# One query tile in the opening, one bounds test at a group's end, and two key tiles of values a visit, in an attention and bilinear-GLU block

## The chip, the cores and the metric

The kernel runs on one core of a Trainium2 chip. The metric is the device time of one execution in microseconds; times are compared as medians of several executions on the same chip. Engines are called as in the profile: PE is TensorE (PEld its weight loads), DVE is VectorE, ACT is ScalarE, POOL is GpSimd, SP is SyncE, which issues all of this kernel's DMAs.

## What is computed

A pre-norm attention with one shared head of keys and values, followed by a pre-norm bilinear GLU, both with a residual. In the reference, cut to what matters:

```python
B, S, D, H, Dh, F = 1, 2048, 576, 32, 18, 4608
q = (ln(x) @ wq).reshape(B, S, H, Dh).transpose(0, 2, 1, 3)
k, v = ln(x) @ wk, ln(x) @ wv                       # one head for all 32
scores = einsum("bhqd,bkd->bhqk", q, k) * Dh ** -0.5
o = einsum("bhqk,bkd->bhqd", softmax(scores), v)
h = x + o.transpose(0, 2, 1, 3).reshape(B, S, H * Dh) @ wo
n = ln(h)
out = h + ((n @ w_gate) * (n @ w_up)) @ w_down
```

## The kernel before

The 2048 rows are taken in four blocks of 512 queries (`TB`), the keys in 16 tiles of 128 (`NT`), the 32 heads in 8 groups of 4 (`NG`). The order of the work is written out by hand; each engine runs its own instructions in the order in which the program emits them, and semaphores hold an instruction until what it reads has been written and the buffer that it writes has been read.

`keys_values` (L141 to L295) is the opening. It loads x, normalises it block by block (`stats`, `scale`, `apply`), transposes each block on PE (`turn`, L200), splits it into a high and a low part (`parts`), projects keys and values (`project`, L220) and finishes the keys (`keys`, L231 to L235). `wq` is split in the same way by `split_wq`. The first block's five tiles of queries (`queries(0)`, 14 matmuls of 128 rows each, L307) stand between these steps.

`queries(b)` (L298) makes the queries of a block in five tiles of up to 7 heads. For the later blocks each of a tile's 14 steps is two matmuls of 64 rows, into two accumulators `psq` and `psr` (L316); DVE adds the two (L322, L323), splits the sum and stores it to DRAM (`q_dram`, L328, L329). `ps_f`, the pool of these accumulators, has two buffers. `bounds` (L336) computes from the absolute values of a block's queries and keys a bound for each query and head of the scores, which is subtracted inside the score matmul; it goes through `m_dram`. `guard` (L348) tests if the largest bound is above a limit; all engines read the flag, and only where it is set the branch computes exact maxima (`exact_maxima`). There are two guards: one for block 0 ahead of the first pair, one for the other blocks.

A pair (`pair`, L434) is two heads against one key tile: two score matmuls (L443) into a buffer `s`, and one exponential on ACT (L445) into a tile `P`. The pool of `s` has two buffers, that of `P` six (`P_BUFS`), later seven. Two pairs make a group's four heads against one key tile; `flush` (L454) multiplies them with the values, four matmuls side by side into `acc` (L460). `load_q`, `load_m` and `prefetch_q` bring a group's queries and bounds back from DRAM. At a group's end `normalise` (L478) turns the sums and divides, `chunk` transposes them, `project(b, c)` (L532) multiplies by `wo`; `run_aux` emits one of these per round.

The first attention's main loop is in `run` (L772 to L781). One visit emits a pair, steps of the other blocks' queries (`STEP` 2, each step counting 1, so two of them), a second pair, one round of `run_aux`, and flushes all waiting key tiles but the newest. When the queries are done and the second guard has run, the visits go on without them (L784 to L788) to the end of block 0's 256 pairs; then `fill` puts further pairs beside the output projection and the second normalisation. From `ffn(0)` (L658) on, the remaining pairs of the 1024 stand between the matmuls of the feed-forward, 8 to each of its 36 hidden tiles.

Of the kernel before, what the change touches and what calls it, by code (L numbers as in the profile page):

```python
# [22 lines left out]
P = 128  # L23
# [32 lines left out]
class Block:  # L56
# [84 lines left out]
    def keys_values(self):  # L141
        pe, act, dve, sp, pool = self.pe, self.act, self.dve, self.sp, self.nc.gpsimd
        with self.tc.tile_pool(name="p0", bufs=1) as p0:
            kvw = self.op.tile([P, S + 5 * P], F32, tag="ob", name="kvw")
            kv, wkv = kvw[:, 0:S], kvw[:, S:].rearrange("p (c m) -> p c m", c=5)
            x01 = [self.hp.tile([P, NQ, D], F32, tag="h", name=f"x{b}") for b in range(2)]
            x23 = self.otp.tile([P, 2, NQ, D], F32, tag="oT", name="x23")
            xs = x01 + [x23[:, 0], x23[:, 1]]
            wqr = [(self.qp if c < 2 else self.qb).tile([P, D], F32, tag="q" if c < 2 else "qs", name=f"wqr{c}")
                   for c in range(4)]  # L150
            for b in range(NB):
                for s in range(NQ):
                    sp.dma_start(xs[b][:, s, :], self.x[b * TB + s * P: b * TB + (s + 1) * P, :])
                if b == 0:
                    sp.dma_start(self.C, self.cst)
                    sp.dma_start(wkv, self.wkv)
                if b == 2:
                    for c in range(4):
                        sp.dma_start(wqr[c], self.wq[:, c, :])
            wqr.append(self.qp.tile([P, D], F32, tag="q", name="wqr4"))  # L160
            sp.dma_start(wqr[4], self.wq[:, 4, :])
            w_h = self.pp.tile([P, 5, P], F32R, tag="P", name="w_h")
            w_l = self.pp.tile([P, 5, P], F32R, tag="P", name="w_l")
            pool.memset(self.V, 0.0)
            pool.memset(self.V[:, :, 0:1], 1.0)
            ksum = p0.tile([P, NB], F32, name="ksum")
            mv = p0.tile([P, NT, 2], F32, name="mv")
            nmean, nmb, kab, kabq = (p0.tile([P, 1], F32, name=n) for n in ("nmean", "nmb", "kab", "kabq"))
            kabs = p0.tile([P, NB], F32, name="kabs")
            ma, mb, mc = (self.C[0:64, c:c + 1] for c in (C_MA, C_MB, C_MC))  # L170
            rs, xhs, trs = {}, {}, []

            def stats(lo, hi):
                for j in range(lo, hi):
                    b, s = divmod(j, NQ)
                    self.ln_stats(xs[b][:, s, :], mv[:, j, :], s, f"a{b}")

            def scale(lo, hi, eng):
                r = self.rstd(mv[:, lo:hi, 1], f"a{lo}", eng, hi - lo)
                n = self.lp.tile([P, hi - lo], F32, tag="n", name=f"n{lo}")  # L180
                eng.tensor_tensor(n, mv[:, lo:hi, 0], r, ALU.mult)
                eng.tensor_scalar(n, n, -1.0, None, ALU.mult)
                for j in range(lo, hi):
                    rs[j] = r[:, j - lo:j - lo + 1], n[:, j - lo:j - lo + 1]

            def apply(b):
                for s in range(NQ):
                    xh = xhs[s] = self.pp.tile([P, 640], F32, tag="P", name=f"xh{b}_{s}")
                    r, n = rs[NQ * b + s]
                    act.activation(xh[:, 0:D], xs[b][:, s, :], AF.Identity, bias=n, scale=r)  # L190
                    pool.tensor_copy(xh[:, D:], xh[:, 512:D])

            def turn(b):

                tail = self.ps_m(f"trt{b}")
                for r in range(2):
                    tr = self.ps_s(f"tr{b}_{r}").rearrange("p a (c q) -> p (a c) q", q=2 * P)
                    for s in (2 * r, 2 * r + 1):
                        for c in range(5):
                            pe.transpose(tr[:, c, (s - 2 * r) * P:(s - 2 * r + 1) * P] if c < 4 else tail[:, s * P:(s + 1) * P],  # L200
                                         xhs[s][:, c * P:(c + 1) * P], self.ident)
                        del xhs[s]
                    trs.append((b, r, tr))
                trs.append((b, None, tail))

            def parts():

                while trs:
                    b, r, tr = trs.pop(0)
                    XT = self.XT[b]  # L210
                    if r is None:
                        self.split_tail(XT[:, 8, :], tr)
                    else:
                        sl = slice(2 * r * P, (2 * r + 2) * P)
                        self.split(XT[:, 0:4, sl], XT[:, 4:8, sl], tr)

            def project(b):
                psk = self.ps_a(f"psk{b}")
                for i, (w, m) in enumerate(passes(w_h, w_l, self.XT[b])):
                    pe.matmul(psk, w, m, start=(i == 0), stop=(i == 13))  # L220
                act.activation(kv[:, b * TB:(b + 1) * TB], psk, AF.Copy, accum_out=ksum[:, b:b + 1])

            def keys(b):

                sl = slice(b * TB, (b + 1) * TB)
                if b == 0:
                    dve.tensor_scalar(nmean, ksum[:, 0:1], -1.0 / TB, None, ALU.mult)
                    dve.scalar_tensor_tensor(nmb[0:64], nmean[0:64], mb, mc, ALU.mult, ALU.add)
                kk = self.pp.tile([P, 2, TB], F32R, tag="P", name=f"kk{b}")
                hi, k2 = kk[0:64, 0], f32(kk[0:64, 1])  # L230
                act.activation(hi, kv[0:64, sl], AF.Identity, bias=nmean[0:64])  # L231
# [3 lines left out]
                dve.tensor_reduce(kabs[0:64, b:b + 1], f32(self.kT[0:64, sl]), AX.X, ALU.max, apply_absolute_value=True)  # L235

            first = self.queries(0)

            def first_queries():
                for _ in range(14):  # L240
                    next(first)

            def split_wq(c):
                act.copy(self.wq_h[:, c], wqr[c])
                pool.tensor_tensor(self.wq_l[:, c], wqr[c], f32(self.wq_h[:, c]), ALU.subtract)

            stats(0, 4)
            scale(0, 4, dve)
            apply(0)
            stats(4, 8)  # L250
            scale(4, 8, pool)
            turn(0)
            stats(8, 10)
            parts()
            split_wq(0)
            apply(1)
            stats(10, 12)
            scale(8, 12, pool)
            split_wq(1)
            turn(1)  # L260
            stats(12, 16)
            scale(12, 16, pool)
            self.split(w_h, w_l, wkv)
            project(0)
            parts()
            apply(2)
            for c in (2, 3, 4):
                split_wq(c)
            turn(2)
            project(1)  # L270
            parts()
            keys(0)
            apply(3)
            turn(3)
            parts()
            first_queries()
            keys(1)
            project(2)
            first_queries()
            first_queries()  # L280
            keys(2)
            project(NB - 1)
            first_queries()
            keys(NB - 1)
            first_queries()
            psv = self.ps_a("psv")
            for t in range(NT):
                pe.transpose(psv[:, t * 32:t * 32 + DH], kv[64:64 + DH, t * P:(t + 1) * P], self.ident[64:64 + DH, 64:64 + DH])
            dve.tensor_reduce(kab[0:64], kabs[0:64], AX.X, ALU.max)
            psb = self.ps_m("psb")  # L290
            pe.matmul(psb[:, 0:1], self.C[0:64, C_SEL:C_SEL + P], kab[0:64], start=True, stop=True)
            dve.tensor_copy(kabq, psb[:, 0:1])
            dve.tensor_scalar(self.G, self.C[:, C_G:C_G + 64], kabq, None, ALU.mult)
            drain(first)
            act.copy(self.V[:, :, 1:1 + DH], psv.rearrange("p (t c) -> p t c", c=32)[:, :, 0:DH])  # L295
# [52 lines left out]
    def guard(self, blocks, name):  # L348
# [10 lines left out]
        for _ in range(4):  # L359
            yield STEP  # L360
# [551 lines left out]
```

## Time and profile before

| | us |
|---|---|
| median of 3 runs | 2430.37 (2430.13 to 2431.2) |
| profiled execution | 2431.05, its span 2428.9 |
| PE busy | 2365.0, 97% of the span |
| ACT busy | 1241.3, 51% |
| DVE busy | 978.8, 40% |
| opening, to the first pair | 0 to 89.6 |
| first attention, to the feed-forward | 89.6 to 437 |
| feed-forward with pairs, then without | 437 to about 1914, about 1914 to 2428.9 |

A row of the timeline gives the start in us from the span's start, the duration, the engine, the source line, the operation, the tile written and the tiles read, the shape, how many instructions were merged (x), and in brackets how long the engine had been idle and what ended that. Matmuls overlap: a row's duration is longer than the time from its start to the next one's, and only the latter adds up. In the counts of L460 a tile of values is x8 (four matmuls, each executed in two passes). A row of a table by stage gives for each engine the busy time and the number of instructions, then the granted PE clock, the DMA share and GB/s.

### The profile page before, as it was taken

What the parts mean: (1) busy time and instruction counts of PE and PEld (TensorE: products, weight loads), DVE (VectorE), ACT (ScalarE), POOL (GpSimd) and SP (SyncE); (2) the same over time, 40 slices, a digit from 0 to 9 for tenths busy, and PEclk for the clock granted to TensorE, in tenths of its full rate; (3) what the DMA queues carried; (4) which work ended last, traced back from release to release, by engine and by line L of the source; (5) the groups of instructions that cost most, each with busy time, mean ns of one, the idle gap of its engine ahead of it and who ended that gap; (6) DMA issues with size and microseconds to landing.
All of it is one profiled execution on the core that took longest, in us unless ns stands there. A gap on an engine that the chain in (4) does not pass through costs nothing.

```text
span 2428.9 us, 44073 instructions
## 1 busy us (share of the span) xinstructions
PE 2365.0 (97%) x18778; PEld 1659.3 (68%) x18778; DVE 978.8 (40%) x1679; ACT 1241.3 (51%) x1396; POOL 354.8 (15%) x409
## 2 busy tenths in 40 slices
PE   5899989999999999999999999999999999999999
PEld 4433424576667667776767776767767778888888
DVE  5222224243334344443333344433333464554454
ACT  4588877746565655556465546466564401111110
POOL 4000000111111111111111111111111112222221
PEclk8899999999999999999999999999999999999999
DMA  3322130312211222422122122232221213423321
GB/s 114 113 64 67 56 112 18 97 57 72 72 62 59 85 62 62 147 67 70 45 73 71 62 62 80 87 113 77 67 67 45 79 65 104 146 89 103 98 89 59
DMA packets 68694, 190.59 MB, mean 78 GB/s; under 512 B 7720, under 2 KB 7848, under 8 KB 68488
## 3 DMA queue, kind: packets, MB, share of 16 engines
q1 hardware_dynamic: 68488, 187.66, 24.4%
q8 instruction: 152, 2.49, 0.4%
q14 instruction: 54, 0.44, 0.1%
HBM read 159.39 MB, written 19.40 MB: 74 GB/s over the span
## 4 chain that ended last, share of the span: by engine, by line
PE 83%; DVE 1%; ACT 1%; issue 0%; ACTq 0%; DVEq 0%
PE pg L678 23%; PE y L651 19%; PE acc L460 15%; PE gu L678 12%; PE s L443 9%; PE yo L547 3%; PE pu L678 1%; PE pt L486 1%; ACT P L445 1%; PE to L134 0%; PE tx L596 0%; DVE ws L86 0%; DVE hf L697 0%; ACT g L693 0%; DVE bsb L100 0%
## 5 line engine op out<-in xcount | busy, mean ns | idle before, releaser
L445 ACT ACTIVATE P<-s 128x1024 f32<-128x1024 f32 x1024 | 1034.2, 1025 | 654.5 <-PE s L443 567.4
L678 PE MATMUL pg<-X,ws 64*128 64x512 f32 x2538 | 700.3, 393 | 0.0
L678 PE MATMUL pu<-X,ws 64*128 64x512 f32 x2538 | 700.3, 393 | 0.0
L678 PEld LDWEIGHTS pg<-X,ws 64*128 64x128 f32 x2538 | 469.7, 186 | 108.1 <-issue 6.5
L460 PE MATMUL acc<-P,V 128*32 128x512 f32 x4096 | 492.6, 600 | 0.7 <-ACT P L445 0.6
L678 PEld LDWEIGHTS pu<-X,ws 64*128 64x128 f32 x2538 | 469.3, 186 | 4.1
L651 PE MATMUL y<-wds,ha 128*128 128x288 f32 x2304 | 465.4, 297 | 2.7 <-ACT ha L85 1.2
L443 PE MATMUL s<-q,kT 56*128 56x512 f32 x2048 | 435.9, 423 | 16.1 <-DVEq L365 12.8
L651 PEld LDWEIGHTS y<-wds,ha 128*128 128x128 f32 x2304 | 369.6, 188 | 26.8 <-issue 23.5
L443 PEld LDWEIGHTS s<-q,kT 56*128 56x128 f32 x2048 | 194.2, 185 | 218.5 <-ACT P L445 114.0
L651 PE MATMUL y<-wds,hl 128*128 128x288 f32 x1152 | 340.8, 296 | 0.1
L678 PE MATMUL gu<-X,ws 64*128 64x512 f32 x2700 | 314.3, 390 | 2.2 <-DVE ws L86 2.2
L85 POOL CAST ws<-wr 128x1152 fp32r<-128x1152 f32 x144 | 166.0, 1153 | 965.6 <-PE pu L678 684.8
L678 PEld LDWEIGHTS gu<-X,ws 64*128 64x128 f32 x2700 | 252.7, 185 | 58.3 <-issue 3.4
L460 PEld LDWEIGHTS acc<-P,V 128*32 128x32 f32 x4096 | 114.1, 109 | 246.4 <-issue 231.8
L697 DVE TENSOR_TENSOR hf<-pu,g 128x512 f32<-128x512 f32 x94 | 65.0, 691 | 528.8 <-ACT g L693 528.8
L653 DVE TENSOR_TENSOR h<-h,y 128x288 f32<-128x288 f32 x384 | 172.9, 453 | 257.3 <-PE y L651 257.1
L693 ACT COPY g<-gu 128x512 f32<-128x512 f32 x50 | 29.3, 587 | 389.4 <-PE gu L678 389.4
L85 POOL CAST wds<-wdr 128x576 fp32r<-128x576 f32 x144 | 146.2, 1034 | 510.3 <-PE y L651 503.4
L651 PEld LDWEIGHTS y<-wds,hl 128*128 128x128 f32 x1152 | 216.8, 188 | 0.4 <-DVE hl L86 0.4
L86 DVE TENSOR_TENSOR ws<-wr,ws 128x1152 fp32r<-128x1152 f32 x144 | 205.8, 1429 | 0.0
L86 DVE TENSOR_TENSOR hl<-hf,ha 128x512 fp32r<-128x512 f32 x144 | 100.8, 700 | 149.4 <-ACT ha L85 149.4
(144 smaller groups left out, 1272.7 us busy)
## 6 DMA issues: line engine op xcount, KB each, us to landing
wr<-in_wgu_dram SPq DMA_DIRECT2D x144, 576.0 KB
wdr<-in_wd_dram SPq DMA_DIRECT2D x144, 288.0 KB
q<-q_dram SPq DMA_DIRECT2D x64, 216.0 KB
q_dram<-qs SPq DMA_DIRECT2D x16, 504.0 KB
X<-X SPq DMA_DIRECT2D x28, 256.0 KB
x<-in_x_dram SPq DMA_DIRECT2D x16, 288.0 KB
h<-in_x_dram SPq DMA_DIRECT2D x16, 288.0 KB
out_dram<-h SPq DMA_DIRECT2D x16, 288.0 KB
```

Of the source, the lines that this page charges most:

```text
L85: (copy or self.cast)(hi, src)
L86: self.dve.tensor_tensor(lo, src, f32(hi), ALU.subtract)
L443: self.pe.matmul(s_[:, i], self.kT[o:o + 56, t * P:(t + 1) * P], self.q[o:o + 56, pr], start=True, stop=True)
L445: self.act.activation(p_, s_, AF.Exp, scale=SCALE)
L460: self.pe.matmul(self.acc[32 * j:32 * j + 32, :], self.V[:, t, :], Ps[j // 2][:, j % 2, :], start=(t == 0), stop=(t == NT - 1), skip_group ...
L486: pe.transpose(pt[:, s * P:(s + 1) * P], os_[:, s * P:(s + 1) * P], self.ident)
L547: pe.matmul(y[:, :HD], m, k, start=(i == 0), stop=(i == len(ms) - 1))
L651: pe.matmul(y[:, :HD], m, w, start=(i == 0), stop=(i == len(ms) - 1))
L653: dve.tensor_tensor(hs, hs, y[:, :HD], ALU.add)
L678: pe.matmul(ps, w[o:o + 64, wk, c], X[o:o + 64, xk, c], start=(j == 0), stop=(j == 26))
L693: act.copy(g, pg)
L697: dve.tensor_tensor(hf, pu, g, ALU.mult)
```

## The change

**The opening.** `keys_values` splits `wkv` first, loads `wq` ahead of the third block of x, and reads the key projection straight from PSUM: `project` no longer copies it by ACT. For block 0 `mean` makes the copy on ACT; for the others DVE makes it, in the second half of `keys`. The doubling of the last 64 columns (`twice`) becomes its own step on DVE or POOL, and a block's tail is transposed after its other parts. Only the first of block 0's five query tiles is made here; its bounds and the first group's queries follow at once, and there is no guard.

```diff
             def project(b):
-                psk = self.ps_a(f"psk{b}")
+            psk = psks[b] = self.ps_a(f"psk{b}")
                 for i, (w, m) in enumerate(passes(w_h, w_l, self.XT[b])):
                     pe.matmul(psk, w, m, start=(i == 0), stop=(i == 13))
-                act.activation(kv[:, b * TB:(b + 1) * TB], psk, AF.Copy, accum_out=ksum[:, b:b + 1])
+        def mean():
+            act.activation(kv[:, 0:TB], psks[0], AF.Copy, accum_out=ksum)
...
+        def keys(b):
...
+            act.activation(hi, psks[b][0:64], AF.Identity, bias=nmean[0:64])
+            dve.tensor_reduce(kabs[0:64, b:b + 1], f32(hi), AX.X, ALU.max, apply_absolute_value=True)
+            def rest():
+                if b:
+                    dve.tensor_copy(kv[:, sl], psks[b])
...
+        apply(1)
...
+        project(0)
+        parts()
+        apply(2)
+        twice(dve)
+        mean()
+        turn(2)
+        project(1)
+        parts()
+        keys(0)()
+        split_wq(2)
+        apply(3)
+        twice(pool)
+        late = keys(1)
+        split_wq(3)
+        split_wq(4)
+        turn(3)
+        late()
+        project(2)
+        parts()
+        for _ in range(14):
+            next(first)
+        next(first)
+        q = self.qt[0, 0] = self.qp.tile([P, 2, TB], F32R, tag="q", name="q0_0")
+        self.load_q(q, 0, 0)
+        keys(2)()
+        project(3)
+        late = keys(3)
...
+        self.bounds(0, act.copy)
+        self.load_m(q, 0, 0)
+        late()
...
+        return first
```

**Queries and bounds.** The other four tiles of block 0 are made as the later blocks' are, in steps of two matmuls. The sum of the two accumulators is made in the tile `qs` itself, since block 0's input is still needed where it lay before. `bounds` takes whatever tiles are ready; block 0's come tile by tile, and `known[b]` says how many heads have them. `prefetch_q` loads a group's queries when these heads cover it, and asks at every key tile from the third on.

```diff
-            if b == 0:
+            if b == i == 0:
...
-                    if b > 1 and i == 0 and k == 5:
-                        self.bounds(b - 1)
+                    if k == 5 and self.tqs and self.tqs[0][0] < max(b, 1):
+                        self.bounds(self.tqs[0][0])
...
-                t = self.p0q.tile([P, 2, TB], F32, tag="XT0", name=f"qt{b}_{i}")
-                dve.tensor_copy(t[:r, 0], psr[:r])
-                dve.tensor_tensor(t[:r, 1], psq[:r], t[:r, 0], ALU.add)
-                self.split(qs[:r, 0], qs[:r, 1], t[:r, 1], dve.tensor_copy)
+                t = f32(qs[:r, 0])
+                dve.tensor_copy(t, psr[:r])
+                dve.tensor_tensor(f32(qs[:r, 1]), psq[:r], t, ALU.add)
+                dve.tensor_copy(qs[:r, 0], f32(qs[:r, 1]))
+                dve.tensor_tensor(qs[:r, 1], f32(qs[:r, 1]), f32(qs[:r, 0]), ALU.subtract)
...
-        if b == NB or not self.queried >= b:
+        if b == NB or (b, g) in self.qt or self.known[b] < 4 * g + 4:
             return
...
-            if t == 2:
+            if t >= 2:
                 self.prefetch_q(b, g + 1)
```

**The visits and the guard.** A visit holds four pairs. Each pair adds `RATE` 1.25 to what is due of the query steps, so a visit has five of them. At its end all waiting key tiles but the newest are flushed, two a visit. `flag` computes the test when all queries are done; `guard` branches on it at the end of the group in which that happens, with all key tiles flushed. If the flag is set, the exact maxima are computed and `again` repeats the groups done so far.

```diff
-                    others, live = rest(), True
+                    others, live, due = rest(), True, 0.0
                     while live:
-                        self.pair()
-                        due = STEP
-                        while due > 0 and live:
-                            z = next(others, None)
-                            live = z is not None
-                            due -= z or 0
-                        self.pair()
+                        for i in range(4):
+                            self.pair()
+                            due += RATE
+                            while due > 0 and live:
+                                z = next(others, None)
+                                live = z is not None
+                                due -= z or 0
                         self.run_aux(1)
                         self.flush(len(self.pend) - 1)
+            self.flag()
             self.wp, self.hh, self.p2 = pool("w", 2), pool("hid", 4), pool("P2", 1)
             self.load_wo_0()
-            while self.more(0):
-                self.pair()
-                self.pair()
-                self.run_aux(1)
-                self.flush(len(self.pend) - 1)
+            self.steps(lambda: self.n_pair % (2 * NT))
+            self.flush(len(self.pend))
+            self.guard()
+            self.wo_from = self.n_pair + 12
+            self.steps(lambda: self.more(0))
...
+    def steps(self, on):
+        while on():
+            for i in range(4):
+                self.pair()
+            self.run_aux(1)
+            self.flush(len(self.pend) - 1)
...
+RATE = 1.25
```

The scores and the values of a pair move into helpers of their own (`scores`, `values`), which emit the same instructions. For block 0 the divisor is clamped from below before its reciprocal (one DVE operation more in each group).

More of the change, by code (lines that the diff above doesn't have):

```diff
@@ new lines, in parts, with project @@
+        def parts():
+            while trs:
+                b, r, tr = trs.pop(0)
+                XT = self.XT[b]
+                if r is None:
+                    self.split_tail(XT[:, 8, :], tr)
+                else:
+                    sl = slice(2 * r * P, (2 * r + 2) * P)
+                    self.split(XT[:, 0:4, sl], XT[:, 4:8, sl], tr)
+        def project(b):
+            psk = psks[b] = self.ps_a(f"psk{b}")
+            for i, (w, m) in enumerate(passes(w_h, w_l, self.XT[b])):
+                pe.matmul(psk, w, m, start=(i == 0), stop=(i == 13))
@@ L294, in keys_values, with split_wq @@
-            drain(first)
-            act.copy(self.V[:, :, 1:1 + DH], psv.rearrange("p (t c) -> p t c", c=32)[:, :, 0:DH])
+            return rest
+        first = self.queries(0)
+        def split_wq(c):
+            act.copy(self.wq_h[:, c], wqr[c])
+            pool.tensor_tensor(self.wq_l[:, c], wqr[c], f32(self.wq_h[:, c]), ALU.subtract)
+        act.copy(w_h, wkv)
+        pool.tensor_tensor(w_l, wkv, f32(w_h), ALU.subtract)
+        stats(0, 4)
+        scale(0, 4, dve)
+        apply(0)
@@ new lines, in again @@
+    def again(self, g):
+        q = self.pp.tile([P, 2, TB], F32R, tag="P", name=f"qa{g}")
+        self.load_q(q, 0, g)
+        self.load_m(q, 0, g)
+        acc = self.ps_a(f"acca{g}")
+        for t in range(NT):
+            Ps = []
+            for pr in range(2):
+                s_ = self.ps_s(f"sa{g}_{t}_{pr}")
+                p_ = self.pp.tile([P, 2, TB], F32, tag="P", name=f"Pa{g}_{t}_{pr}")
+                self.scores(s_, p_, q, t, pr)
+                Ps.append(p_)
+            self.values(acc, Ps, t)
+            del Ps, p_, s_
+        os_ = self.os.get(g)
+        if os_ is None:
+            os_ = self.pp.tile([P, TB], F32, tag="P", name=f"osa{g}")
+        self.dve.tensor_copy(os_, acc)
+        if g not in self.os:
+            self.normal_heads(0, g, os_)
```

366 lines of the change are left out of this document (166 added, 200 removed).

## The prediction

> **What bounds the kernel now.** I read the page first, then its busy time by stage, then the timeline of the stage that the change rewrites.
>
> ```profile
> span 2428.9 us, 44073 instructions
> ...
> PE 2365.0 (97%) x18778; PEld 1659.3 (68%) x18778; DVE 978.8 (40%) x1679; ACT 1241.3 (51%) x1396; POOL 354.8 (15%) x409
> ```
>
> ```profile
> core 0: us, PE busy (x) PEld busy (x) DVE busy (x) ACT busy (x) POOL busy (x), PEclk, DMA share, GB/s
> ...
> 89.60:339.00 249.40, 247.21 (x1784) 97.24 (x1784) 66.19 (x129) 213.35 (x220) 0.00 (x0) 0.98 0.19 61
> ...
> 351.00:437.00 86.00, 82.33 (x530) 36.35 (x532) 36.10 (x94) 62.34 (x67) 3.94 (x6) 0.97 0.17 56
> 437.00:1680.00 1243.00, 1241.28 (x10187) 879.88 (x10183) 481.41 (x812) 720.70 (x792) 178.58 (x177) 1.00 0.24 76
> ```
>
> Over the whole span PE is the bound, and from 437 us on (the feed-forward) it is so without a gap: whatever is moved there costs its PE time. The average hides the stage from 89.6 to 437 us, the first attention, where ACT's exponentials take 213 of 249 us: two engines stand close to their limit, and each visit's order decides which one waits. One visit of before, with queries beside the pairs:
>
> ```profile
> 229.41 0.50 PE L443 MATMUL s<-q,kT 56*128 56x512 f32 x2
> 229.74 0.39 PE L316 MATMUL psq<-XT,wq_h 64*126 64x512 f32 x1
> ...
> 229.98 0.40 PE L316 MATMUL psq<-XT,wq_l 64*126 64x512 f32 x1
> ...
> 230.22 0.40 PE L443 MATMUL s<-q,kT 56*128 56x512 f32 x2
> 230.54 1.06 PE L460 MATMUL acc<-P,V 128*32 128x512 f32 x8
> 231.54 0.50 PE L443 MATMUL s<-q,kT 56*128 56x512 f32 x2
> ...
> 232.11 0.39 PE L316 MATMUL psr<-XT,wq_l 64*126 64x512 f32 x1
> ...
> 232.54 0.69 DVE L322 COPY qt<-psr 126x512 f32<-126x512 f32 x1 [11.77 <-PE psr L316]
> ...
> 233.27 0.69 DVE L323 TENSOR_TENSOR qt<-psq,qt 126x512 f32<-126x512 f32 x1
> ```
>
> From start to start: a score pair before a query step 0.33, a query step 0.24, score pair to values 0.32, one key tile of values 1.00. Sum 0.33 + 0.24 + 0.24 + 0.32 + 1.00 = 2.13 us for two pairs and two steps, all of it PE. Where no queries are left:
>
> ```profile
> 361.16 0.90 PE L443 MATMUL s<-q,kT 56*128 56x512 f32 x4
> 361.77 3.77 ACT L445 ACTIVATE P<-s 128x1024 f32<-128x1024 f32 x4 [0.25 <-PE s L443]
> 361.99 1.07 PE L460 MATMUL acc<-P,V 128*32 128x512 f32 x8
> 362.99 0.51 PE L443 MATMUL s<-q,kT 56*128 56x512 f32 x2
> 363.76 0.49 PE L443 MATMUL s<-q,kT 56*128 56x512 f32 x2 [0.27 <-ACT P L445]
> 364.19 1.06 PE L460 MATMUL acc<-P,V 128*32 128x512 f32 x8
> 365.18 0.91 PE L443 MATMUL s<-q,kT 56*128 56x512 f32 x4
> ```
>
> Here ACT sets the pace. An exponential starts 0.60 after its scores (361.16 to 361.77); the next one 0.92 after it ((3.77 - 1.02) / 3, 1.02 being one). The score buffers are two: the scores at 363.76 waited for the second exponential (started 361.77 + 0.92 = 362.69), so a buffer is free 1.07 after its exponential starts. Two scores and a tile of values take 0.41 + 0.42 + 1.00. Chained by these rules, two visits take 4.02 us; the rows have 365.18 - 361.16 = 4.02. The rules hold, and I use them for the changed order.
>
> **Four pairs a visit.** The changed visit is: scores, step, step, scores, step, scores, step, scores, step, two tiles of values. What a second tile of values costs behind the first, and what a pair costs within the feed-forward, these rows show:
>
> ```profile
> 442.27 0.39 PE L678 MATMUL pg<-X,ws 64*128 64x512 f32 x1
> ...
> 442.50 0.41 PE L443 MATMUL s<-q,kT 56*128 56x512 f32 x2
> 442.73 0.39 PE L678 MATMUL pg<-X,ws 64*128 64x512 f32 x1
> ...
> 443.30 2.78 PE L460 MATMUL acc<-P,V 128*32 128x512 f32 x24
> 446.01 0.50 PE L678 MATMUL pg<-X,ws 64*128 64x512 f32 x1
> ```
>
> Three tiles take 2.71, so each further one costs (2.71 - 1.00) / 2 = 0.86 and batching saves 0.14. Now the chain, from the first scores at 0. Exponential 0 starts at 0.60. Scores 1 at 0.33 + 2 x 0.24 = 0.80; exponential 1 at 0.60 + 0.92 = 1.52. Scores 2 could start at 0.80 + 0.33 + 0.24 = 1.37, but their buffer is free only at 0.60 + 1.07 = 1.67; exponential 2 at 2.44. Scores 3 could start at 2.24 and wait until 1.52 + 1.07 = 2.59; exponential 3 at 3.36. Last step, then values from about 3.18, 1.86 long: the next visit starts at 5.05. ACT's last work of the visit ends at 4.38, its next starts at 5.65: it starves during the two tiles of values, because only two score buffers' worth of work can lie in front of it, and PE has waited 0.30 + 0.35 for it before. Before spends 4 pairs and 5 steps in 2 x 2.13 + 0.24 = 4.50. Per visit the change loses 0.55, though its pure PE work is 4.40. Without steps the same chain gives 4.87 against 4.02.
>
> [...]
>
> **Tile boundaries.** A query tile's two accumulators are its only ones. The next tile's second accumulator is free when DVE has copied one and added the other: 233.27 + 0.69 + 0.05 - 232.11 = 1.90 after the last step. Before, 14 steps are seven visits, so the boundary always falls behind the values, which hide it (0.24 + 0.32 + 1.00 + 0.33 = 1.89). After, 14 steps against 5 a visit put it at every place in turn. Between two steps with scores between them PE comes back after 0.92 (ACT's pace), 0.98 short, of which 0.33 were waited for ACT anyway: 0.65. Adjacent steps lose about 1.0, the place across the values nothing. Mean (3 x 0.65 + 1.0 + 0) / 5 = 0.6; bounds 0 and 1.0. There are 19 tiles, 18 boundaries: 11 us (0 to 18). Everything on PE queues behind the waiting step: scores first, then ACT.
>
> **The opening.**
>
> ```profile
> 29.16 0.60 ACT L221 ACTIVATE kvw<-psk 128x512 f32<-128x512 f32 x1 [4.91 <-PE psk L220]
> ...
> 42.68 0.60 ACT L221 ACTIVATE kvw<-psk 128x512 f32<-128x512 f32 x1 [5.80 <-PE psk L220]
> ...
> 49.19 1.11 PE L200 MATMUL tr<-C,xh 128*128 128x128 f32 x4 [6.55 <-ACT xh L190]
> ...
> 53.20 0.71 PE L307 MATMUL psq<-XT,wq_h 128*126 128x512 f32 x2
> ...
> 56.55 0.63 PE L220 MATMUL psk<-XT,w_h 128*128 128x512 f32 x2
> ```
>
> ```profile
> 81.12 0.33 SPq L344 DMA_DIRECT2D m_dram<-m  x1
> ...
> 82.37 0.14 DVE L358 TENSOR_SCALAR flaga<-mx2a 1x1 int32<-1x1 f32 x1
> ...
> 83.77 1.15 SPq L380 DMA_DIRECT2D q<-m_dram  x4
> ...
> 89.63 0.89 PE L443 MATMUL s<-q,kT 56*128 56x512 f32 x2 [7.51 <-DVEq L365]
> ```
>
> ACT twice stood before a key projection it had to copy (4.91 + 5.80), with the next block's normalisation queued behind it, for which PE then waited at 49.19. The change puts those copies later or on DVE: -10.7 (between -5.8, if another queue holds the block, and -14). Four tiles of queries leave, each 56.55 - 53.20 = 3.3: -13.2. They are not removed: as 56 steps they are in the stretch below. New: the last key projection waits until the third is read, which now stands behind the first query tile's evacuation; one ACT pass of 0.6 and four DVE passes of 0.69 as in the row at 232.54: +3.4 (0 to 5). The removed first guard: PE waited for its branch until 89.63. The bounds' way stays: write issued 81.12, reload issued 83.77, and landing, estimated at the write's 2.3 (81.45 to 83.77), gives 86.1, so -3.5. First pair: 89.6 - 10.7 - 13.2 + 3.4 - 3.5 = 65.6 us, between 61 and 71. SP's queue gets the kT copies behind the reload; the first pairs need only block 0's, issued long before.
>
> **The guard, and the sum.**
>
> ```profile
> 344.98 0.49 PE L443 MATMUL s<-q,kT 56*128 56x512 f32 x2
> ...
> 350.75 0.79 PE L443 MATMUL s<-q,kT 56*128 56x512 f32 x2 [5.27 <-DVEq L365]
> ```
>
> ```profile
> L322 DVE COPY qt<-psr x15: 677/691/693, 104.3 to 326.9; 126x512 f32<-126x512 f32 x12, 72x512 f32<-72x512 f32 x3
> ```
>
> One guard of 5.77 stays (344.98 to 350.75); its larger skipped body I take as free, both guards of before costing PE about as much. Flushing every tile ahead of it adds one tile, 0.86.
>
> 1. First pair: -24.0.
> 2. Stretch with queries. Before: 89.6 to 326.9, 237.3 us for 210 pairs; 105 visits x 2.13 are 223.7, the other 13.6 are normalisation, bounds and start-up. After: 19 x 14 = 266 steps, 53.2 visits of 5.05: 268.7, + 13.6 + 11 = 293.3. Difference +56.0.
> 3. To the end of the guard. Before 326.9 to 350.75, 17 pairs: 23.9. After 11 pairs at 4.87 / 4 = 13.4, the same 1.0 of bounds, 0.86 and 5.77: 21.0. Difference -2.9.
> 4. To the feed-forward. Before 86 us for 62 pairs (289 exponentials are issued by then); after 57 (281): three more to pair 256, at the slower rate 32 x 1.22 - 29 x 1.01 = +9.7, then eight fewer beside the projections at about 1.0 and fewer waits there: -11. Difference -1.5 (-5 to +3).
> 5. These eight pairs go to the feed-forward, 442.50 to 442.73 and half of 0.9: 8 x 0.68 = +5.5.
>
> Sum +33.1. The profiled execution took 2431.05 (2.15 beyond its span), 0.7 above the median of 2430.37; I add to the median: **2464 us**. The end of the flag test, the smaller P and query tiles and the loads of queries cost nothing: the flag lies a visit ahead of its guard, and a group's queries are loaded about 12 pairs before use. [...]
>
> **The rivals.** (a) Faster: PE never waits for ACT, because the exponentials catch up during the values. Then visits cost 4.40 (-35), boundaries vanish (-11), the stretch without queries keeps 4.02 (-4): 2414 us. For it: PE is 97% busy. Against it:
>
> ```profile
> PEld s L443 <- ACT P L445: 91.2, 111, 1.4
> ```
>
> Already before, score weights waited 111 times for an exponential between 89.6 and 339 us, by as much as 1.4 us. It decides if ACT's gap at a visit's start stays under 0.6 us. (b) Slower, but less: boundaries hidden by ACT's waits and the opening at its early end, 2464 - 11 - 5 = 2448 us. [...] (d) The change does not do what it says: PE order has only four steps a pair group and one tile, 2430 us; the emitted order excludes most of that.
>
> **How the numbers follow.** Forecast 0.55, its own range 2455 to 2472 (opening and boundaries). (b) 0.25, (c) 0.06, (a) 0.11, (d) 0.03. The range 2440 to 2480 leaves out (a), (d) and little else. A measurement can tell 0.2% (4.9 us) from no change: faster 0.11, same 0.03, slower 0.86.
>
> **What would show it.** First scores near 66 us; visits of about 5.05 us in PE's timeline with score waits of 0.3 twice a visit and an ACT gap of about 1.3 at its start; boundaries where psr waits for DVE; no guard stall before the first pair; first feed-forward matmul near 465. I am wrong if visits stay at 4.4 to 4.5, or if a load of queries or the opening's SP queue holds the first pair beyond 71.

## The result, and the profile after

| | before | after |
|---|---|---|
| median, on the same chip | 2430.78 (4 runs, 2430.13 to 2431.78) | 2472.05 (4 runs, 2469.69 to 2475.69) |
| ratio, with its 95% interval | | 1.0171 (1.0153 to 1.0188) |
| profiled execution, its span | 2431.05, 2428.9 | 2473.66, 2471.9 |

The change costs 41.3 us, 1.7%. The forecast was 2464 us, 33.1 more than before. The page of the changed kernel, its total and its slices:

```profile
span 2471.9 us, 44165 instructions
...
PE 2379.9 (96%) x18833; PEld 1669.0 (68%) x18833; DVE 1000.1 (40%) x1719; ACT 1233.9 (50%) x1385; POOL 356.4 (14%) x402
...
PEclk8899997999999999999999999999999999999999
```

The page alone shows little: PE has 55 instructions more, its busy time grew by 14.9 us, and the span by 43.0, so 28 us are new idle of an engine that is still 96% busy. They have to be looked for by stage. The table by stage (each row begins with start and end in us and the length), with the changed kernel's own borders: first pair, last copy of a query tile, first pair behind the guard, feed-forward:

```profile
51.70:58.00 6.30, 6.07 (x14) 4.43 (x14) 0.74 (x1) 0.13 (x1) 0.72 (x1) 0.55 0.50 158
...
65.70:368.70 303.00, 270.18 (x1850) 107.97 (x1850) 82.41 (x158) 201.83 (x213) 0.00 (x0) 0.98 0.19 60
368.70:391.30 22.60, 13.95 (x85) 4.04 (x83) 11.36 (x17) 11.24 (x12) 4.61 (x5) 0.86 0.56 179
391.30:400.00 8.70, 7.03 (x24) 2.44 (x24) 0.00 (x0) 6.16 (x7) 1.15 (x1) 0.50 0.46 171
400.00:420.00 20.00, 18.50 (x100) 8.38 (x98) 4.57 (x14) 10.79 (x12) 0.00 (x0) 0.78 0.00 1
420.00:440.00 20.00, 17.44 (x110) 9.50 (x114) 5.16 (x12) 12.99 (x14) 0.00 (x0) 0.91 0.00 0
...
480.50:2467.80 1987.30, 1979.42 (x16248) 1489.51 (x16244) 829.15 (x1351) 931.82 (x1056) 322.01 (x313) 1.00 0.25 79
```

The first row is a stretch of the opening, to which the last part returns. Two things are to be seen in the others. In the stretch with queries neither engine is full any more: PE 270 of 303 us (before 247 of 249), ACT 202. The two wait for each other in turn. And from 391 to 440 us the granted clock is below full speed, at 0.50 first. Before, it was low for 8 us behind the guard, in this row, and at 1.00 from 360 us on:

```profile
352.00:360.00 8.00, 7.59 (x40) 2.24 (x32) 3.10 (x9) 4.86 (x6) 0.77 (x1) 0.70 0.60 211
```

The timeline of one plain visit, from its first scores (196.48) to the next visit's (201.59), then a visit in which a group ends:

```profile
196.48 0.50 PE L502 MATMUL s<-q,kT 56*128 56x512 f32 x2
...
197.09 3.77 ACT L503 ACTIVATE P<-s 128x1024 f32<-128x1024 f32 x4 [1.05 <-PE s L502]
...
198.16 0.50 PE L502 MATMUL s<-q,kT 56*128 56x512 f32 x2 [0.24 <-ACT P L503]
...
199.08 0.50 PE L502 MATMUL s<-q,kT 56*128 56x512 f32 x2 [0.18 <-ACT P L503]
...
199.74 1.92 PE L507 MATMUL acc<-P,V 128*32 128x512 f32 x16
201.59 0.50 PE L502 MATMUL s<-q,kT 56*128 56x512 f32 x2
...
202.22 3.77 ACT L503 ACTIVATE P<-s 128x1024 f32<-128x1024 f32 x4 [1.36 <-PE s L502]
...
206.01 0.69 DVE L518 COPY os<-acc 128x512 f32<-128x512 f32 x1 [10.97 <-PE acc L507]
206.75 1.07 PE L507 MATMUL acc<-P,V 128*32 128x512 f32 x8 [0.81 <-DVE os L518]
207.75 0.50 PE L502 MATMUL s<-q,kT 56*128 56x512 f32 x2
```

A plain visit takes 201.59 - 196.48 = 5.11 us. PE waits for ACT twice (0.24 and 0.18 of idle), and ACT then stands still for 1.36 us while PE is busy with two tiles of values: four exponentials in 5.13 us (197.09 to 202.22), of which ACT works 3.77. The second visit takes 207.75 - 201.59 = 6.16. In it the last key tile of a group and the first of the next one are multiplied in one go; they share the one accumulator `acc`, so PE stood until DVE had copied it (206.01 + 0.69). Before, these two tiles fell into different visits, with scores and query steps between them.

### The profile page after: what moved, and what is told of

The parts are those of the page before. It is cut to its first block, busy times and chain, and to the rows that moved or that the text cites. A ratio compares the mean times of both kernels' runs of the same rounds, so it can differ in the third digit from the quotient of the medians.

```text
span 2471.9 us, 44165 instructions
## 1 busy us (share of the span) xinstructions
PE 2379.9 (96%) x18833; PEld 1669.0 (68%) x18833; DVE 1000.1 (40%) x1719; ACT 1233.9 (50%) x1385; POOL 356.4 (14%) x402
## 5 line engine op out<-in xcount | busy, mean ns | idle before, releaser
L507 PE MATMUL acc<-P,V 128*32 128x512 f32 x4096 | 485.8, 605 | 5.8 <-DVE os L518 5.1
L502 PE MATMUL s<-q,kT 56*128 56x512 f32 x2048 | 442.6, 426 | 34.6 <-ACT P L503 28.2
L743 PE MATMUL gu<-X,ws 64*128 64x512 f32 x2646 | 307.3, 389 | 0.0
L507 PEld LDWEIGHTS acc<-P,V 128*32 128x32 f32 x4096 | 120.8, 110 | 273.1 <-issue 255.4
L762 DVE TENSOR_TENSOR hf<-pu,g 128x512 f32<-128x512 f32 x95 | 65.7, 692 | 526.4 <-ACT g L758 526.4
```

The lines of the kernel that those rows point to most:

```text
L502: self.pe.matmul(s_[:, i], self.kT[o:o + 56, t * P:(t + 1) * P], q[o:o + 56, pr], start=True, stop=True)
L507: self.pe.matmul(acc[32 * j:32 * j + 32, :], self.V[:, t, :], Ps[j // 2][:, j % 2, :], start=(t == 0), stop=(t == NT - 1), skip_group_chec ...
L743: pe.matmul(ps, w[o:o + 64, wk, c], X[o:o + 64, xk, c], start=(j == 0), stop=(j == 26))
L762: dve.tensor_tensor(hf, pu, g, ALU.mult)
```

## The experiments

The time of each kernel, and three lengths from its profiled execution: to the first pair's scores, from there to the first feed-forward matmul, and from there to the last matmul. The number of pairs done before the feed-forward stands in brackets.

| kernel | median us | ratio to before (95%) | opening | first attention | feed-forward |
|---|---|---|---|---|---|
| before | 2430.78 | 1 | 89.6 | 347.3 (288) | 1988.2 |
| after | 2472.05 | 1.0171 (1.0153 to 1.0188) | 65.7 | 414.8 (280) | 1987.3 |
| e1 two pairs a visit | 2433.11 | 1.0006 (0.9997 to 1.0016) | 63.1 | 374.0 (280) | 1988.8 |
| e2 before, four pairs a visit | 2483.04 | 1.0209 (1.0194 to 1.0225) | 90.6 | 397.2 (288) | 1989.4 |
| e3 tiles end with visits | 2462.66 | 1.0125 (1.0109 to 1.0140) | 66.0 | 403.2 (280) | 1987.3 |
| e4 two pairs without queries | 2469.23 | 1.0152 (1.0138 to 1.0166) | 65.9 | 406.8 (280) | 1985.7 |
| e5 two pairs, tiles end with visits | 2422.98 | 0.9957 (0.9943 to 0.9971) | 66.3 | 364.5 (280) | 1986.7 |
| e6 as e5, no guard | 2413.58 | 0.9922 (0.9907 to 0.9937) | 65.6 | 354.0 (280) | 1988.4 |
| e7 eight more pairs | 2479.63 | 1.0198 (1.0183 to 1.0214) | 66.1 | 423.1 (288) | 1984.9 |
| e8 values of one tile | 2433.36 | 1.0004 (0.9995 to 1.0013) | 65.7 | 373.3 (280) | 1988.7 |
| e9 after, no guard | 2464.26 | 1.0134 (1.0117 to 1.0151) | 65.9 | 407.2 (280) | 1988.7 |

Kernels run at different times are compared by their ratios, each to the kernel before on its own chip.

**e1 and e8: what the visit costs.** Two edits that leave opening, moved queries and guard alone. The first halves the visit, in both loops:

```diff
-            for i in range(4):
+            for i in range(2):
                 self.pair()
```

> The changed kernel with two pairs a visit instead of four, everywhere in the first attention, so that values are multiplied one key tile a visit; opening, moved queries, one late test of bounds and the rate of query steps stay (1.25 steps a pair, counted over two pairs). Theory: what the change loses, it loses because two key tiles of values in one go leave ScalarE waiting for scores. Then the visits fall from 5.1 us to about 2 x 2.1 = 4.3 us with queries and from 4.9 to about 4.0 us for four pairs without; the opening's 24 us stay gained, some 10 us go for the moved steps, bounds and boundaries: about 2422 us, 0.990 to 1.000 of before. Rival: the moved query tiles, their boundaries and the late guard cost what is lost, whatever the size of a visit: 2455 us or more.

The second keeps the visit of four pairs with its other work at the end, and only takes a tile of values forward (the same two lines stand in `steps`):

```diff
                                 due -= z or 0
+                            if i == 1:
+                                self.flush(len(self.pend) - 1)
                         self.run_aux(1)
                         self.flush(len(self.pend) - 1)
```

> The changed kernel with its visits of four pairs, their other work once a visit and its rate of steps, but the values of one key tile multiplied after each two pairs instead of two tiles' values at the end. Theory: it is the eight value matmuls in one go that leave ScalarE without scores (and put a group's end and the next one's start into one wait): about 2433 us, as with two pairs a visit. Rival: it is the visit of four pairs as such, with its other work at its end: about 2465 to 2472 us.

Both bring back about 40 of the 41 us, and e8 lands on its theory's figure. So it is neither the length of the visit nor how often its other work runs, but two tiles of values in one go. The timeline of e8, a visit with the same four pairs and five steps:

```profile
204.79 0.50 PE L502 MATMUL s<-q,kT 56*128 56x512 f32 x2
...
205.39 1.94 ACT L503 ACTIVATE P<-s 128x1024 f32<-128x1024 f32 x2 [0.19 <-PE s L502]
...
206.16 1.06 PE L507 MATMUL acc<-P,V 128*32 128x512 f32 x8
207.15 0.50 PE L502 MATMUL s<-q,kT 56*128 56x512 f32 x2
...
207.75 1.94 ACT L503 ACTIVATE P<-s 128x1024 f32<-128x1024 f32 x2 [0.42 <-PE s L502]
...
209.28 0.51 PE L502 MATMUL s<-q,kT 56*128 56x512 f32 x2
```

209.28 - 204.79 = 4.49 us, against 5.11; ACT's idle is 0.19 + 0.42 instead of 1.36 (or 1.05), and no score of PE waits for it. e1 missed its theory's 2422 by 11 us. The boundaries are most of that. The 18 visits of e1 in which the copy of a finished tile starts took 3.37 us on the mean by the timeline, where plain visits take 2.13 with two steps and 2.36 with three: about 20 us in all, of which two other operations in these visits take 1.2. The expectation had 10 for moved steps, bounds and boundaries together. (The expectation of e5, below, has 3.03 against 2.14, 16 us; counted by the visit in which the copy starts, it is more.) e5 takes the boundaries up.

**e2: the same edit on the kernel before.** There, the loop body with its two pairs and their steps runs twice before `run_aux` and `flush`, and likewise in the loop without queries.

```diff
                     while live:
-                        self.pair()
-                        due = STEP
...
-                        self.pair()
+                        for i in range(2):
+                            self.pair()
+                            due = STEP
...
+                            self.pair()
                         self.run_aux(1)
                         self.flush(len(self.pend) - 1)
```

> The kernel before, with four pairs a visit instead of two in both loops of the first attention, so that two key tiles of values are multiplied a visit; nothing else. Theory: the four-pair visit by itself costs the whole loss and more. In the query stretch a visit of four pairs goes from 4.26 to about 4.8 us (some 52 of them: 27 us), without queries some 10 us more, and each of seven group ends with the next group's start in one visit 1 us: about 2473 us (1.012 to 1.020). Rival: the size of a visit is nothing, the matmuls are the same: 2430 us.

It lost 51 us, more than the changed kernel. Seen by stage, from the first pair to the last query matmul it took 270.7 us against 236.8: +33.9, the 27 + 6 of the theory. The surplus over the theory's 2473 lies behind the queries: 126.5 against 110.5 us up to the feed-forward, +16 where 10 and one more group's end were expected. The timeline there:

```profile
410.79 0.50 PE L443 MATMUL s<-q,kT 56*128 56x512 f32 x2 [0.95 <-ACT P L445]
411.70 0.78 PE L443 MATMUL s<-q,kT 56*128 56x512 f32 x2 [0.41 <-ACT P L445]
412.41 3.27 PE L460 MATMUL acc<-P,V 128*32 128x512 f32 x16
...
419.14 3.13 PE L547 MATMUL yo<-wo,oT 128*128 128x288 f32 x12
...
422.87 1.92 PE L460 MATMUL acc<-P,V 128*32 128x512 f32 x16
```

Two tiles of values take 3.27 us here and 1.92 us ten us later: PE runs slower, though the matmuls are the same. This is the low clock of the stage table again, in another kernel with four pairs a visit: from 404 to 424 us e2's granted clock was 0.74.

**e3 and e5: where a query tile ends.** The steps are dealt out so that a tile's 14th step is a visit's last, with visits of four pairs (e3) and of two (e5).

```diff
+                        steps, visits = (5, 5, 4, 5, 5, 4, 7, 7)[visits % 8], visits + 1
...
-                            due += RATE
-                            while due > 0 and live:
...
+                            for _ in range(steps // 4 + (i < steps % 4)):
+                                live = live and next(others, None) is not None
```

> The changed kernel with the same visits of four pairs, but the steps of queries dealt out so that every query tile ends where a visit ends, and never in the middle of one. Theory: a boundary inside a visit makes TensorE wait for the new tile's PSUM banks while ScalarE runs dry, 0.6 to 0.9 us for each of 11 boundaries; with the boundary at the end, the values of the visit cover it: about 2462 us, 0.4% under the changed kernel. Rival: a boundary is paid wherever it lies, or the wait only moves: 2472 us, as the changed kernel.

e3 came to 2462.66, as its theory had it; the ratios differ by 0.0046, about 11 us. In its list of waits there is no row left of PE's matmuls waiting for DVE at a tile's accumulators, and PE's weight loads wait there for 2.5 us in all; the changed kernel has, from 65.7 to 368.3 us (total, times, longest):

```profile
ACT P L503 <- PE s L502: 103.9, 68, 5.2
...
PE s L502 <- ACT P L503: 18.9, 82, 0.5
...
PE acc L507 <- DVE os L518: 5.0, 6, 0.9
PE psq L338 <- DVE qs L344: 4.6, 7, 0.8
PE psr L338 <- DVE qs L345: 3.7, 15, 0.3
```

The 11 us are not the price of the boundaries alone. By the timelines, the 18 visits of the changed kernel in which the copy of a finished tile starts took 20.1 us more than 18 x 5.11; without two group ends and two other operations that fall into them, about 17. The same visits of e3 took no longer than others. But e3 also packs the steps closer, 42 in eight visits against 40: its queries end at 340.8 us instead of 368.3, with nine pairs fewer done, and these stand in the stretch behind, which grew from 112.2 to 128.4 us.

For e5 the visit has two pairs, and the steps after its two pairs are listed, 28 steps (two tiles) in eleven visits:

```diff
+                        steps = ((1, 1), (2, 1), (1, 1), (2, 1), (1, 1), (2, 0),
+                                 (2, 1), (2, 1), (2, 1), (2, 1), (2, 0))[visits % 11]
...
+                        for n in steps:
                             self.pair()
...
+                            for _ in range(n):
+                                live = live and next(others, None) is not None
```

> The changed kernel with two pairs a visit everywhere and the steps of queries dealt out so that every query tile ends behind the first pair of a visit: a score pair and one key tile of values stand between its last matmul and the next tile's first. Theory: of what the two-pair kernel still loses against its opening's gain, the boundaries are the larger part (its 18 visits with a boundary's copies took 3.03 us on the mean, the plain ones 2.14: 16 us); ended this way they cost at most a third: 2421 to 2424 us, 0.4% under before. Rival: with two pairs a visit the boundary's copies are too long for what covers them and the wait moves only: 2431 us or more, as before.

At 2422.98 us, ratio 0.9957 (0.9943 to 0.9971), e5 is faster than both kernels, 8.9 us under before and, by the ratios, about 12 under e1. Its opening keeps its gain (66.3 us). PE's waits for a new tile's first accumulator are a third of e1's in number and 0.4 of them in time. The row in the list of waits of e5, from 66.3 to 322.4 us, and that of e1, from 63.1 to 333.6 us:

```profile
PE psq L338 <- DVE qs L344: 2.8, 4, 1.0
```

```profile
PE psq L338 <- DVE qs L344: 7.2, 12, 0.8
```

**e6 and e9: the guard, and the clock behind it.** The line `self.guard()` is left out, from e5 and from the changed kernel. Neither kernel has the branch that recomputes the first attention from exact maxima.

> The same kernel as the two-pair one whose tiles end with visits, without the late guard: the flag is still computed, but the branch that recomputes the first attention's maxima exactly is left out, with its wait. It prices the guard: the branch, the wait of all engines and the half clock behind it. Theory: 7 us in which TensorE stands still and 4 us lost to half clock for the 8 us behind: 10 to 12 us less, about 2411 us. Rival: the wait behind the branch is for the weights' transfers, which come no sooner: 5 us less, about 2417 us.

> The changed kernel, its visits of four pairs kept, without the late guard: the flag is still computed, but the branch that recomputes the maxima exactly, and its wait, are left out. Theory: the half clock until about 426 us is set off by TensorE standing still in the guard and then kept up by the short idles of the four-pair visits; without the guard the clock stays near 1.00 there, and 11 us of guard plus some 6 us of slow matmuls go: about 2455 us. Rival: the short idles of the four-pair visits alone halve the clock; the cold stretches stay where they are or come in other places, and only the guard's own 9 us go (what the two-pair kernel without it gained): about 2463 us.

e6 gained 9.4 us on e5 (2413.58 against 2422.98), just under its theory's 10 to 12 and well over the rival's 5. e9 gained 7.8 us on the changed kernel, its rival's 2463 within 1.3. What tells most about the clock is e9's timeline, in which no branch stands anywhere:

```profile
371.84 0.50 PE L502 MATMUL s<-q,kT 56*128 56x512 f32 x2 [0.70 <-ACT P L503]
372.76 0.50 PE L502 MATMUL s<-q,kT 56*128 56x512 f32 x2 [0.42 <-ACT P L503]
373.19 3.42 PE L507 MATMUL acc<-P,V 128*32 128x512 f32 x16
...
380.50 1.92 PE L507 MATMUL acc<-P,V 128*32 128x512 f32 x16
...
389.92 0.50 PE L502 MATMUL s<-q,kT 56*128 56x512 f32 x2 [0.98 <-ACT P L503]
...
399.40 0.50 PE L502 MATMUL s<-q,kT 56*128 56x512 f32 x2 [0.94 <-ACT P L503]
400.32 0.50 PE L502 MATMUL s<-q,kT 56*128 56x512 f32 x2 [0.41 <-ACT P L503]
400.75 3.25 PE L612 MATMUL yo<-wo,oT 128*128 128x288 f32 x12
...
406.99 1.88 PE L612 MATMUL yo<-wo,oT 128*128 128x288 f32 x12
```

The same two tiles of values take 3.42 us at 373.19 and 1.92 at 380.50, the same twelve matmuls 3.25 and 1.88. PE had not stood still for longer than 0.98 us at once between 366 and 400; the visits just before the slow rows had 0.70 + 0.42 and 0.94 + 0.41 us of idle. So the clock was low in four-pair visits where there is no guard: 0.89 from 368 to 384 us and 0.83 from 400 to 420. It wasn't in each of them: from 390 to 400 us, with the longest idle of all at its start, e9's clock was full:

```profile
390.00:400.00 10.00, 7.34 (x46) 2.52 (x46) 1.87 (x8) 8.06 (x9) 1.15 (x1) 1.00 0.82 282
```

What decides between such visits isn't shown by these runs. The half clock of the expectations, e4's below among them, was 0.50 in e1 for the 8 us behind its branch (356 to 364) and in the changed kernel from 391 to 403 us; from 391 to 426 us the latter had 0.70 on the mean. With one tile of values at a time PE is nearly without idle. The table by stage of e8, 15 to 35 us behind its branch (350.7), where the changed kernel (branch at 383.6) had 0.78:

```profile
366.00:386.00 20.00, 19.20 (x128) 9.14 (x120) 5.92 (x18) 15.40 (x17) 0.00 (x0) 0.99 0.00 1
```

**e4: two pairs a visit only behind the queries.** The edit of e1 in the helper `steps` alone.

> The changed kernel with two pairs a visit only after the last query (some 57 pairs around and behind the guard), four as long as queries run. Theory: the 27 us at half clock behind the guard come from the idle of the four-pair visits there, of which two-pair visits have none: 12 us for shorter visits by the durations at full clock (4.9 to 4.0 us for four pairs), and some 5 us more from the clock: about 2455 us, with the clock at full by 405 us. Rival: the clock falls because TensorE stands still for the guard, whatever follows: about 2463 us, with the same cold stretches until about 425 us.

The clock is at 1.00 from 402 us on, as the theory had it, and in the profiled execution the stretch from the last query to the feed-forward shrank from 112.2 to 104.3 us. But the median is 2469.23, above both forecasts, and the ratios of e4 and the changed kernel overlap (1.0138 to 1.0166, 1.0153 to 1.0188). The profiled execution of e4 was its fastest (2464.37), that of the changed kernel one of its slower ones. So the trace shows where the low clock ends; what ending it is worth by itself stays unmeasured.

**e7: eight pairs ahead of the feed-forward instead of beside it.**

```diff
+            for _ in range(8):
+                self.pair()
+                if not self.half:
+                    self.flush(len(self.pend) - 1)
             while self.n_pair % 8 != 4:
```

> The changed kernel with eight more pairs ahead of the feed-forward part, which so begins at as many as in the kernel before (the pairs themselves are the same, eight fewer are left to run beside the feed-forward matmuls). Theory of the prediction: a pair beside the feed-forward matmuls costs TensorE its 0.68 us of matmuls, so the feed-forward part gets 5.5 us shorter, against 8 to 9 us more ahead of it: about 2475 us, the feed-forward part 1982 us. Rival: these eight cost nothing there: about 2480 us, the feed-forward part 1987 us.

The time is the rival's, 2479.63; the feed-forward part came to 1984.9 us, 2.4 under the changed kernel's, between the two. Kernels with the same 280 pairs ahead of it differ among themselves by as much (1985.7 to 1988.8), so a price per pair can't be read from this; against any of them it comes out below the 0.68 us that was assumed.

## Why the prediction was right, and where it was not

The direction, the cause and the range (2440 to 2480) held; the narrower range that the forecast gave itself, 2455 to 2472, ends where the median lies. By its five steps, changed kernel against before, from the two profiled executions:

| step | predicted | measured |
|---|---|---|
| 1. to the first pair | -24.0 | -23.9 (89.63 to 65.69) |
| 2. stretch with queries | +56.0 | +65.7 (303.0 against 237.3) |
| 3. to the end of the guard | -2.9 | -1.3 (22.6 against 23.9) |
| 4. to the feed-forward | -1.5 | +3.0 (89.2 against 86.2) |
| 5. feed-forward | +5.5 | -0.9 (1987.3 against 1988.2) |
| sum | +33.1 | +42.6 |

That the sum comes out within 10 us is in part luck. The first feed-forward matmul, forecast near 465 us, came at 480.5; the fifth step, 6.4 us too dear, took back a part of that.

**The four-pair visit** was the right mechanism at nearly the right size: 5.11 us against the chained 5.05, with both waits of PE and ACT's gap (1.36 against about 1.3) where the chain had put them. Counted as the chain does, from the start of the step before (197.52 and 198.50) plus 0.24, the waits are 0.40 and 0.34 us, forecast 0.30 and 0.35. e8 showed the other end of it: with one tile of values at a time the visit is 4.49, the forecast's 4.50 for the kernel before. Rival (a), in which PE never waits for ACT, falls: its scores waited 82 times between 65.7 and 368.3 us (18.9 us), and taking the batches apart (e8) gained about 40 us. So does (d): the visit at 196.48 has its five steps and its two tiles. That the batches don't pay has the reason that the chain gave: two buffers of scores can't keep ACT busy for two tiles of values. No run has more of these buffers, so that part of the cause is the chain's, and not tried.

**The boundaries** were forecast at 11 us, between 0 and 18. The visits of the changed kernel have about 17 (see e3); that e3 as a whole came out 11 us lower is a coincidence with the forecast. The timeline has one that splits a visit as the prediction put it, between two steps:

```profile
190.83 0.50 PE L502 MATMUL s<-q,kT 56*128 56x512 f32 x2
...
191.40 0.39 PE L338 MATMUL psq<-XT,wq_l 64*126 64x512 f32 x1
...
191.84 0.69 DVE L344 COPY qs<-psr 126x512 f32<-126x512 f32 x1 [11.48 <-PE psr L338]
...
192.59 0.45 PE L338 MATMUL psq<-XT,wq_h 64*72 64x512 f32 x1 [0.56 <-DVE qs L344]
...
193.31 0.45 PE L338 MATMUL psr<-XT,wq_h 64*72 64x512 f32 x1 [0.28 <-DVE qs L345]
```

The next tile's second accumulator was written 1.91 us after the last step, forecast 1.90. The visit took 196.48 - 190.83 = 5.65 us, 0.54 over a plain one, forecast 0.65 for this place. Rival (b), which hid the boundaries, falls with these visits and with e3.

**What step 2 lacked** is 9.7 us. Visits 0.06 us longer make 53 x 0.06 = 3.2. One term was left out altogether: two key tiles in one go also means the end of one group and the start of the next, and `acc` has one buffer. Six group ends of 6.16 - 5.11 = 1.05 each are 6.3. These two add up to nearly 9.7, but only because two other misses cancel: the boundaries took about 6 us more than forecast, and what is left for normalisation, bounds and start-up is about 8 us, where 13.6 had been carried over from before. The prediction costed the second tile of values by a row within the feed-forward, and didn't ask at which pairs the two tiles belong to different accumulators. In e8's list no matmul on `acc` waits for `os` (six in the changed kernel, 5.0 us); PE's weight loads still wait a little:

```profile
PEld acc L507 <- DVE os L518: 2.1, 5, 0.6
```

**Step 4** missed by 4.5 us (its own terms, +9.7 and -11, give -1.3 and not -1.5). Its pairs were costed at full clock, which is the likely reason. The stage table has 0.50 to 0.91 from 391 to 440 us. In the stretch with queries, with waits of about 0.2 us, the clock had 0.98 on the mean. Behind the branch a visit has longer idles, but they alone don't decide: 0.93 and 0.42 us (at 420.78 and 421.70) came before twelve matmuls of 2.88 us, 0.94 and 0.41 us (at 435.52 and 436.43) before the same twelve in 1.89, at a clock of 1.00. That 4.5 us is the clock and nothing else wasn't separated: e4, made for that, was unclear.

**Step 5** was wrong in its price: pairs beside the feed-forward were costed at their PE time, and neither the comparison with before nor e7 finds 5.5 us for eight of them. Why a pair costs less there stays open.

**Step 1** was right by compensation. These timeline rows of the opening show the last key projection and the way of the bounds:

```profile
51.70 1.19 PE L225 MATMUL psk<-XT,w_h 128*128 128x512 f32 x2 [3.28 <-DVE kvw L243]
...
57.87 0.68 ACT L238 ACTIVATE kk<-psk,nmean 64x512 fp32r<-64x512 f32 x1 [8.25 <-PE psk L225]
...
62.32 0.27 SPq L372 DMA_DIRECT2D m_dram<-m  x1
...
65.69 1.01 PE L502 MATMUL s<-q,kT 56*128 56x512 f32 x2 [0.20 <-DMA q<-m_dram]
```

The wait for the third block's evacuation is there (3.28, forecast 3.4). But the projection behind it ran at a clock of 0.55 (the stage table's first row) and took 6.2 us until ACT could read it (51.70 to 57.87), where a query tile of 14 passes had taken 3.3 before. Against that, the bounds came back 3.4 us after their write was issued (62.32 to 65.69) where 5.0 had been allowed (81.12 to 86.1); where the remaining 1.2 us were gained wasn't traced. That some of this is chance shows in e1, whose opening is the same code: its page gives the clock the digit 9 in the first slice of the span (about 61 us), where the changed kernel's has 8, and its first pair came at 63.1 us.

**The change as a whole** is two changes of opposite sign. With the batching of the values taken out (e8) nothing measurable is left of the loss (1.0004, 0.9995 to 1.0013): the opening's 24 us pay for the moved queries, their boundaries and what remains. With the boundaries put where values cover them (e5) the moved queries cost less than the opening gains, and the whole is 0.4% faster than before. The guard costs 8 to 9 us in either order of visits (e6, e9).

## What to carry to other kernels

Before batching work on one engine, chain a single iteration by hand: here what the other engine could do meanwhile followed, by the chain, from the two score buffers between them, and not from the share of busy time. When two tiles are put into one go, look also at the iterations where they belong to different accumulators. Work moved into a loop as steps should have its boundaries fall where other work covers them: the same steps dealt out differently, and packed a little closer, were worth 11 to 12 us here by the ratios, more than the net gain of the version that wins.

## What was not expected of the hardware

PE's granted clock was below full in four-pair visits that held no single idle above 0.98 us, in a kernel without any branch, each of these idles ended by ACT (e9: 0.89 from 368 to 384 us, 0.83 from 400 to 420; the same 16 matmul rows in 3.42 and in 1.92 us). Visits of 5.1 us with two idles of about 0.2 us kept 0.98 (the changed kernel, 65.7 to 368.7). A low clock doesn't come with each such visit: e9 had 1.00 from 390 to 400 us with idles of up to 0.98 us, the changed kernel 1.00 from 435 to 440 us with 0.94 and 0.41. In the opening of the changed kernel the last key projection ran at 0.55 behind an idle of 3.28 us. In e2 the twelve matmuls of the output projection at 419.14 took 3.13 us, and the two tiles of values at 422.87, with no idle of PE between, 1.92.
